# Sorting the second mixture's experts earlier in the program, and one layer 1 output ahead of the weight subtractions

## The chip, the cores and the metric

The kernel runs on one core of one Trainium2 chip. The metric is the device time of one execution in microseconds; the figure for a kernel is the median of several runs. In the profile PE is the matrix engine TensorE (PEld its weight loads), DVE is VectorE, ACT is ScalarE, POOL is GpSimd, and SP issues most of the weight transfers.

## The reference, cut to what matters

An attention without softmax comes first, then two mixtures of eight experts, each of which sends every token to one expert:

```python
kv = np.einsum('bhsd,bhse->bhde', k, v)
out = np.einsum('bhsd,bhde->bhse', q, kv)          # then an RMS norm: x, 2304 tokens of 512
...
xc = x[x @ w_skip > 0]                             # first mixture: the others pass unchanged
e_idx = np.argmax(xc @ w_gate, axis=1)             # gate_w is the softmax at e_idx
for e in range(8):
    h = np.maximum(xc[mask] @ w1[e], 0.0)          # 512 to 1024
    y[mask] = gate_w[mask, None] * (h @ w2[e])     # 1024 to 512
out[do_compute] = xc + y
...
# second mixture: all tokens again, its own gate and weights, a capacity for each expert
h = np.maximum(np.einsum('ecd,edf->ecf', disp, w1), 0.0)
y = np.einsum('ecf,efd->ecd', h, w2)
out[i] = gate_w[i] * y[expert_idx[i], pos[i]]
```

## The kernel before, in words

The rows of all tokens lie in DRAM (`xcat`). A mixture works through eight **slots**; each slot is one expert, the experts sorted by how many tokens they have, and holds up to a fixed number of tokens (`CAP1`, `CAP2`: 384 to 272 in the second mixture). For a slot, POOL gathers the token rows with indirect DMAs of 128 rows (`gather`, L426, index table `gi`), PE transposes them, layer 1 makes `hp` in PSUM, ACT and DVE take it out, layer 2 follows, and POOL scatters the result.

The second mixture multiplies with numbers split in two: ACT casts the high part (`whi` of a weight, `xh` of a row, `hh` of a hidden value), DVE subtracts to get the low part (`wlo` L1159 or L1304, `xl`, `hl` L1330), and PE makes three products (L1310 to L1312). A weight half is 128 x 2048 floats (1,048,576 bytes) in one of six buffers `wraw`; it is cast and subtracted in four pieces of 512 columns.

The expert with most tokens, the **lead**, is known ahead of the others, and its slot 0 runs early, at the end of the first mixture. `l1_early(fc)` makes the eight parts of its layer 1 for the first 256 tokens, and `h_early` takes two parts out at a time. `lead_tokens` makes the index table of its last 128 tokens, `t2_rest` gathers and transposes those, and `l1_rest` makes their layer 1 (L1377) in four pairs of parts. All these `hp` share a pool `p1h` of two PSUM buffers, so the fourth pair of `l1_rest` can start only when the second has been taken out by both ACT (`hh`, L1329) and DVE (`hl`, L1330). Between the early parts stand the last slot's bookkeeping matmuls: `next(todo)` and `run(todo)` step through `add_tokens`, which adds the last tokens to the tables in the PSUM tile `acc` (L1073): A and Bo to the index table `ips2`, U and V to `ups`, which only the overflow path at the end uses.

`sort_experts` then orders the other seven experts, `by_slot` makes their index tables, and `slot_reg` loads the order into the queues. After that `fetch2` may gather the rows of the next slot (three gathers on POOL) and load its four weight halves; for the slot next after the lead these loads stand on POOL's queue behind the gathers, for the others on SP's.

Only PE's order is the order of the code (`manual_schedule`). On DVE, ACT, POOL and SP a scheduler orders the instructions by priority, which follows the code, and by when it thinks them ready; `behind(a, b)` forces `a` after `b`. On the chip each engine then runs its list in that order.

In the first mixture's last slot (j = 7) layer 1 is `l1(j, fp)` for fp 0 to 3. Its outputs for odd fp are taken out by DVE (L711). Right behind the last of them stand `t2_early` (transposes of the lead's first rows, `xl` L1324) and `split2(0, 0)`, the first weight half of the lead, then layer 2, `l2` (L737).

Of the kernel before, what the change touches and what calls it, by code (L numbers as in the profile page):

```python
# [11 lines left out]
ALU = mybir.AluOpType  # L12
# [31 lines left out]
def blocks(n):  # L44
    return [(r, min(128, n - r)) for r in range(0, n, 128)]
# [3 lines left out]
def moe_kernel(ctx: ExitStack, tc: tile.TileContext, qT, kk, vv, aux, w1a, w2a, w1b, w2b, capacity, out):  # L49
    nc = tc.nc  # L50
# [264 lines left out]
    def run(gen):  # L315
        for _ in gen or ():
            pass
# [89 lines left out]
    def slot_reg(order, j, both):  # L407
        eng = [mybir.EngineType.SP] + ([mybir.EngineType.Pool] if both else [])
        return nc.values_load(order[0:1, j:j + 1], engines=eng, min_val=0, max_val=E - 1,
                              skip_runtime_bounds_check_because="the index of an expert")  # L410
# [243 lines left out]
    W, X, XT, HT, YT, GT, EV, YP, LG, YR, XC = {}, {}, {}, {}, {}, {}, {}, {}, {}, {}, {}  # L654
# [28 lines left out]
    def l1(j, fp, c0=0, c1=None, early=False, ffs=(0, 1)):  # L683
        n = CAP1[j]
        c1 = c1 or n
        if fp == 0 and c0 == 0:
            HT[j] = m1.tile([128, 8, 2, n], F32R, name="hT1") if j in SPLIT1 else m1.tile([128, 8, c1], F32, name="hT1")
        if fp == 0 and c0 > 0:
            HT[j] = [m2s.tile([128, 8, c1 - c0], F32R, name=i) for i in ("hh", "hl")]
        if 0 in ffs:  # L690
            YP["hp"] = p1h.tile([128, 2, c1 - c0], F32, name="hp1")
        hp = YP["hp"]
        for ff in ffs:
            fc = fp * 2 + ff
            wv = W[j][fc // 4].rearrange("p (f k m) -> p f k m", f=4, k=4)
            for k in range(4):
                nc.tensor.matmul(hp[:, ff, :], lhsT=wv[:, fc % 4, k, :], rhs=XT[j][:, k, c0:c1], start=(k == 0), stop=(k == 3))  # L697
        if 1 not in ffs:
            return
        if j in SPLIT1:  # L700
            hh, hl = (HT[j][:, 2 * fp:2 * fp + 2, i, :] for i in range(2))
            EV[j] = nc.scalar.activation(out=hh, in_=hp, func=AF.Relu)
            ev = nc.vector.scalar_tensor_tensor(out=hl, in0=hp, scalar=0.0, in1=hh.bitcast(F32), op0=ALU.max, op1=ALU.subtract)
        elif c0 > 0:
            hh, hl = (h[:, 2 * fp:2 * fp + 2, :] for h in HT[j])
            EV[j] = nc.scalar.activation(out=hh, in_=hp, func=AF.Relu)
            EV["rest"] = nc.vector.scalar_tensor_tensor(out=hl, in0=hp, scalar=0.0, in1=hh.bitcast(F32), op0=ALU.max, op1=ALU.subtract)
        elif fp % 2 == 0 or j == 0:
            EV[j] = nc.scalar.activation(out=HT[j][:, 2 * fp:2 * fp + 2, c0:c1], in_=hp, func=AF.Relu)
        else:  # L710
            ev = nc.vector.tensor_scalar(out=HT[j][:, 2 * fp:2 * fp + 2, c0:c1], in0=hp, scalar1=0.0, scalar2=None, op0=ALU.max)  # L711
        if fp == 1 and not early:
            GT[j] = sm.tile([128, NB1], F32, name="g1")
            for bi, (r0, nn) in enumerate(blocks(n)):
                gates(GT[j][:, bi:bi + 1], X[j][bi], nn, D, (None, EV[j]) if j == 0 else (ev, EV[j]))
# [348 lines left out]
    with first_mix:  # L1064
# [86 lines left out]
        def split(raw, after=None, first=None):  # L1151

            hi, lo = pair()
            for c in range(0, 2048, SPLIT):
                cs = slice(c, c + SPLIT)
                ins = nc.scalar.copy(out=hi[:, cs], in_=raw[:, cs])  # L1156
                if first is not None:
                    behind(ins, first)
                ins = nc.vector.tensor_tensor(out=lo[:, cs], in0=raw[:, cs], in1=hi[:, cs].bitcast(F32), op=ALU.subtract)  # L1159
                if after is not None:  # L1160
                    behind(ins, after)
            return hi, lo
# [121 lines left out]
        def split2(j, pc, after=None):  # L1284
            if j in ROWS2 and pc >= 2:
                rows_split(j, pc, after)
            else:
                WS[j, pc] = split(W2[j][pc], after)
# [48 lines left out]
        def l1_early(fc):  # L1337
            xh, xl = XT2[0]
            if fc == 0:
                h_tiles(0)  # L1340
            if fc % 2 == 0:
                YP["h"] = p1h.tile([128, 2, 256], F32, name="hp1")
            hp = YP["h"]
            wv = [w.rearrange("p (f k m) -> p f k m", f=4, k=4) for w in WS[0, fc // 4]]
            for k in range(4):
                mm3(hp[:, fc % 2, :], [w[:, fc % 4, k, :] for w in wv], (xh[:, k, :], xl[:, k, :]), k == 0, k == 3)
            YP["h", fc // 2] = hp

        def h_early(fp):
            ev = h_out(0, YP["h", fp], slice(2 * fp, 2 * fp + 2), slice(0, 256))  # L1350
            if fp == 3:
                GT2[0] = sm.tile([128, NB2], F32, name="g2")
                for bi in range(2):
                    gates(GT2[0][:, bi:bi + 1], X2[0][bi], 128, D + 8, ev)

        def t2_rest():
            n = CAP2[0] - 256
            (x,), _ = load_x(n, r2["gi"], 0, 2)
            X2[0].append(x)
            tp = p1t.tile([128, 4, n], F32, name="tp1")  # L1360
            for dc in range(4):
                nc.tensor.transpose(tp[:, dc, :], x[:n, dc * 128:dc * 128 + 128], ident[:n, :n])
            xB = m2s.tile([128, 4, n], F32, name="xB")
            nc.scalar.copy(out=xB[:, 0:2], in_=tp[:, 0:2])
            nc.vector.tensor_copy(out=xB[:, 2:4], in_=tp[:, 2:4])
            XT2["rest"] = xB

        def l1_rest():
            n = CAP2[0] - 256
            xB = XT2["rest"]  # L1370
            for fp in range(4):
                hp = p1h.tile([128, 2, n], F32, name="hp1")
                for ff in range(2):
                    fc = 2 * fp + ff
                    wv = W2[0][fc // 4].rearrange("p (f k m) -> p f k m", f=4, k=4)
                    for k in range(4):
                        nc.tensor.matmul(hp[:, ff, :], lhsT=wv[:, fc % 4, k, :], rhs=xB[:, k, :], start=(k == 0), stop=(k == 3))  # L1377
                ev = h_out(0, hp, slice(2 * fp, 2 * fp + 2), slice(256, CAP2[0]))
                if fp == 0:
                    gates(GT2[0][:, 2:3], X2[0][2], n, D + 8, ev)  # L1380
# [15 lines left out]
        for j in range(1, E):  # L1396
            l1(j, 0)
            if j == 1:
                rest_turned()
                others_table()  # L1400
                l1(j, 1)
                logits(0)
                back(0, bis=1)
            else:
                logits(j - 1)
                l1(j, 1)
                back(j - 1)
            todo = back_logits(j - 1)
            next(todo)
            l1(j, 2)  # L1410
            if j == 1:
                XC["half"] = EV[j]
            l1(j, 3)
            split1(j, 2)
            split1(j, 3)
            if j + 1 < E:
                t1(j + 1)
            else:
                t2_early()
                split2(0, 0)  # L1420
            l2(j, 0)
            if j < E - 1:
                next(todo)
            l2(j, 1)
            next(todo)
            if j < E - 1:
                run(todo)
            if j == E - 2:
                early([g for i in range(j) for g in SC[i]])
            if j == E - 1:  # L1430
                split2(0, 1)
                split2(0, 2)
            l2(j, 2)
            if j == E - 2:
                add(cnt2, identb, bump)
            l2(j, 3)
            if j + 2 < E:
                fetch1(j + 2)
# [5 lines left out]
        todo = back_logits(E - 1, True)  # L1444
# [4 lines left out]
        l1_early(2)  # L1449
        next(todo)  # L1450
        lead_tokens(r2, ips2, EQ0, slice(2, 3))
        l1_early(3)
        h_early(1)
        l1_early(4)
        run(todo)
        l1_early(5)
        h_early(2)
        l1_early(6)
        t2_rest()
        l1_early(7)  # L1460
        h_early(3)

        ends = rt.tile([128, E], F32, name="ends")
        nc.vector.tensor_copy(out=ends, in_=cnt2)
        key = rt.tile([128, E], F32, name="key_2")
# [2 lines left out]
        sort_experts(r2, key)  # L1468
        by_slot(r2, ips2.rearrange("p e q b -> p e (q b)"), 1, E)
        reg2 = [None] + [slot_reg(r2["order"], j, j == ORDER2[1]) for j in range(1, E)]  # L1470
        l1_rest()
        nc.vector.tensor_tensor(out=OH2, in0=OHk, in1=ups, op=ALU.add)

# [178 lines left out]
```

## Time and profile before

| what | us |
|---|---|
| median of three runs | 482.91 (482.81 to 484.09) |
| the profiled execution | 483.77 |
| its span in the trace | 482.0 |
| PE busy in the span | 464.6 |

The span is what the trace's times count in, from 0; the profiled execution is 1.77 us longer than its span. A row of a timeline gives start, duration, engine, line, operation, out<-in, count, and in brackets how long the engine stood idle ahead of it and what ended that.

### The profile page before, as it was taken

How to read it: one execution, taken by the hardware profiler on the slowest of the kernel's cores; microseconds unless marked ns; L12 is line 12 of the kernel's file. 1: busy time of each engine (PE TensorE's matmuls, PEld its weight loads, DVE VectorE, ACT ScalarE, POOL GpSimd, SP SyncE). 2: the span in 40 equal slices, each digit the busy share in tenths (PEclk: the TensorE clock that was granted, in tenths of full speed). 3: DMA queues.
4: the chain of work that ended last, by engine and by line, in shares of the span. 5: the costliest groups of instructions: out<-in, count | busy, mean ns of one | idle time of the engine just before them, and what ended most of it. 6: DMA issues, size and time to landing. Idle time of an engine off the chain costs nothing.

```text
span 482.0 us, 10172 instructions
## 1 busy us (share of the span) xinstructions
PE 464.6 (96%) x3797; PEld 440.3 (91%) x3797; DVE 304.3 (63%) x964; ACT 206.9 (43%) x514; POOL 143.5 (30%) x177
## 2 busy tenths in 40 slices
PE   7999987999999999999999999999999999999995
PEld 3888987899999999999888999999999999999985
DVE  2367778986776755439683764756657566776611
ACT  1574663455344231126232553554544544555400
POOL 5585955011302123111261410501506033030201
PEclk9999999999999999999999999999999999999999
DMA  8998958989776965565149965554656566310101
GB/s 280 410 407 299 355 214 275 371 306 312 291 258 211 326 185 195 179 253 205 45 134 420 345 242 175 200 184 154 225 175 196 186 239 209 103 38 0 38 22 41
DMA packets 21386, 104.88 MB, mean 218 GB/s; under 512 B 3323, under 2 KB 3451, under 8 KB 12626
## 3 DMA queue, kind: packets, MB, share of 16 engines
q1 hardware_dynamic: 14032, 76.70, 44.9%
q0 software_dynamic: 7152, 27.40, 16.6%
q8 instruction: 31, 0.51, 0.4%
q14 instruction: 25, 0.20, 0.1%
q10 hardware_dynamic: 146, 0.07, 0.1%
HBM read 92.15 MB, written 12.76 MB: 218 GB/s over the span
## 4 chain that ended last, share of the span: by engine, by line
PE 73%; DVE 6%; DMA 3%; issue 1%; ACT 0%; POOL 0%; POOLq 0%; SPq 0%; ACTq 0%
PE hp L697 12%; PE yp L1310 8%; PE yp L1312 8%; PE yp L1311 8%; PE yp L727 6%; PE hp L1310 6%; PE hp L1311 6%; PE hp L1312 6%; PE yp L728 2%; PE yp L737 2%; PE yt L1545 2%; PE tp L1501 2%; DVE wlo L1159 2%; DMA wraw<-in_w1b 1%; PE tp L677 1%; DMA rows<-xcat,gi 1%
## 5 line engine op out<-in xcount | busy, mean ns | idle before, releaser
L1156 ACT CAST whi<-wraw 128x512 fp32r<-128x512 f32 x152 | 86.0, 619 | 77.8 <-PE yp L1311 30.1
L1159 DVE TENSOR_TENSOR wlo<-wraw,whi 128x512 fp32r<-128x512 f32 x152 | 97.3, 685 | 28.7 <-ACT whi L1156 27.6
L426 POOL DMA_INDIRECT rows<-xcat,gi x40 | 42.2, 1056 | 148.6 <-ACT ex L435 86.1
L1310 PE MATMUL hp<-xh,whi 128*128 128x256 f32 (+7 forms) x256 | 78.8, 308 | 0.3 <-DVE hl L1330 0.3
L1312 PE MATMUL hp<-xh,wlo 128*128 128x256 f32 (+7 forms) x256 | 76.7, 299 | 0.0
L1311 PE MATMUL hp<-xl,whi 128*128 128x256 f32 (+7 forms) x256 | 76.6, 299 | 0.0
L697 PE MATMUL hp<-xT,wraw 128*128 128x148 f32 (+8 forms) x544 | 73.5, 291 | 1.5 <-ACT base L1139 1.5
L697 PEld LDWEIGHTS hp<-xT,wraw 128*128 128x128 f32 x544 | 69.8, 190 | 3.2 <-ACT base L1139 1.6
L1535 POOL DMA_INDIRECT out<-ot,toki x24 | 34.7, 1446 | 84.6 <-DVE su L439 39.5
L1310 PE MATMUL yp<-hh,whi 128*128 128x320 f32 (+5 forms) x192 | 58.8, 306 | 0.0
L1312 PE MATMUL yp<-hh,wlo 128*128 128x320 f32 (+5 forms) x192 | 57.3, 298 | 0.0
L1311 PE MATMUL yp<-hl,whi 128*128 128x320 f32 (+5 forms) x192 | 57.3, 298 | 0.0
L1310 PEld LDWEIGHTS hp<-xh,whi 128*128 128x128 f32 x256 | 48.2, 188 | 0.9 <-DVE hl L1330 0.8
L1311 PEld LDWEIGHTS hp<-xl,whi 128*128 128x128 f32 x256 | 48.3, 189 | 0.0
L1312 PEld LDWEIGHTS hp<-xh,wlo 128*128 128x128 f32 x256 | 48.3, 189 | 0.0
L727 PE MATMUL yp<-hT,whi 128*128 128x352 f32 (+4 forms) x160 | 43.1, 350 | 0.0
L1217 POOL DMA_INDIRECT xcat<-rows,toki x16 | 16.3, 1020 | 84.5 <-DVE mxt L382 82.1
L1329 ACT ACTIVATE hh<-hp 128x320 fp32r<-128x320 f32 (+8 forms) x64 | 27.1, 428 | 32.7 <-PE hp L1312 25.1
L1330 DVE SCALAR_TENSOR_TENSOR hl<-hp,hh 128x320 fp32r<-128x320 f32 (+8 forms) x64 | 30.1, 477 | 13.8 <-ACT hh L1329 12.5
L728 PE MATMUL yp<-hT,wlo 128*128 128x176 f32 (+4 forms) x160 | 37.7, 236 | 0.0
L1311 PEld LDWEIGHTS yp<-hl,whi 128*128 128x128 f32 x192 | 36.2, 188 | 0.0
L1310 PEld LDWEIGHTS yp<-hh,whi 128*128 128x128 f32 x192 | 36.1, 188 | 0.0
(308 smaller groups left out, 856.0 us busy)
## 6 DMA issues: line engine op xcount, KB each, us to landing
wraw<-in_w2a SPq DMA_DIRECT2D x14, 1024.0 KB
wraw<-in_w1b SPq DMA_DIRECT2D x14, 1024.0 KB
wraw<-in_w2b SPq DMA_DIRECT2D x14, 1024.0 KB
wraw<-in_w1a SPq DMA_DIRECT2D x13, 1024.0 KB
xcat<-xa SPq DMA_DIRECT2D x18, 264.0 KB
q<-in_q SPq DMA_DIRECT2D x4, 1152.0 KB
wraw<-in_k SPq DMA_DIRECT2D x8, 512.0 KB
wraw<-in_v SPq DMA_DIRECT2D x8, 512.0 KB
```

The lines of the kernel that those rows point to most:

```text
L426: return nc.gpsimd.indirect_dma_start(out=rows[:n], out_offset=None, in_=xcat[0:source], in_offset=bass.IndirectOffsetOnAxis(ap=gi[:n], ax ...
L697: nc.tensor.matmul(hp[:, ff, :], lhsT=wv[:, fc % 4, k, :], rhs=XT[j][:, k, c0:c1], start=(k == 0), stop=(k == 3))
L727: nc.tensor.matmul(yp, lhsT=wh[:, fc, :], rhs=HT[j][:, fc], start=(fc == 0), stop=False, skip_group_check=True)
L728: nc.tensor.matmul(yp[:, 0, :], lhsT=wl[:, fc, :], rhs=HT[j][:, fc, 0, :], start=False, stop=(fc == 7), skip_group_check=True)
L1156: ins = nc.scalar.copy(out=hi[:, cs], in_=raw[:, cs])
L1159: ins = nc.vector.tensor_tensor(out=lo[:, cs], in0=raw[:, cs], in1=hi[:, cs].bitcast(F32), op=ALU.subtract)
L1310: nc.tensor.matmul(ps, lhsT=wh, rhs=xh, start=first, stop=False)
L1311: nc.tensor.matmul(ps, lhsT=wh, rhs=xl, start=False, stop=False)
L1312: nc.tensor.matmul(ps, lhsT=wl, rhs=xh, start=False, stop=last)
L1329: ea = nc.scalar.activation(out=hh[:, fs, cs], in_=hp, func=AF.Relu)
L1330: ev = nc.vector.scalar_tensor_tensor(out=hl[:, fs, cs], in0=hp, scalar=0.0, in1=hh[:, fs, cs].bitcast(F32), op0=ALU.max, op1=ALU.subtract)
L1535: st = nc.gpsimd.indirect_dma_start(out=out, out_offset=bass.IndirectOffsetOnAxis(ap=r2["toki"][:nn, j, bi:bi + 1], axis=0), in_=ot[:nn], ...
```

## The change

Two edits. `sort_experts`, `by_slot` and the register loads move ahead of the lead's parts 3 to 7 and the gather of its last tokens, right behind `lead_tokens`; the U and V additions (`run(todo)`) go behind part 5. And the last odd output of layer 1 of the last slot (`EV["odd"]`) is handed to `split2(0, 0)`, so that the subtractions of that weight half come behind it on DVE.

```diff
@@ l1 @@
-            ev = nc.vector.tensor_scalar(out=HT[j][...], in0=hp, scalar1=0.0, scalar2=None, op0=ALU.max)
+            ev = EV["odd"] = nc.vector.tensor_scalar(out=HT[j][...], in0=hp, scalar1=0.0, scalar2=None, op0=ALU.max)
...
                 t2_early()
-                split2(0, 0)
+                split2(0, 0, EV["odd"])
...
         lead_tokens(r2, ips2, EQ0, slice(2, 3))
-        l1_early(3)
-        h_early(1)
-        l1_early(4)
-        run(todo)
-        l1_early(5)
-        h_early(2)
-        l1_early(6)
-        t2_rest()
-        l1_early(7)
-        h_early(3)
-
         ends = rt.tile([128, E], F32, name="ends")
...
         reg2 = [None] + [slot_reg(r2["order"], j, j == ORDER2[1]) for j in range(1, E)]
+        l1_early(3)
+        h_early(1)
+        l1_early(4)
+        l1_early(5)
+        run(todo)
+        h_early(2)
+        l1_early(6)
+        t2_rest()
+        l1_early(7)
+        h_early(3)
+
         l1_rest()
```

**On DVE, around the last odd output (L711 of hp_3468).** Here `xl` is the low part of the lead's rows, `wlo` of its weights, A, Bo and V are the tables of the slot before.

```order
+L1116 TENSOR_TENSOR V<-hv,o_1_1243 128x144
 L711 TENSOR_SCALAR hT_3375<-hp_3468 128x272
-L387 TENSOR_SCALAR o_1_1243<-sct,m2t,valid_1612 128x8
+L1159 TENSOR_TENSOR wlo<-wraw,whi 128x512 x2
 L1324 TENSOR_TENSOR xl<-tp_3480,xh 128x512
 L1324 TENSOR_TENSOR xl<-tp_3487,xh 128x512
```

The five L1159 that stood ahead of this L711 in the order (two of them even ahead of the first odd output) are now behind it, two at once and the rest behind `xl`. From there to the copy L741 that layer 2 needs, the list before reads

```order
L1109 TENSOR_TENSOR Bo<-o_1_1243,tab_207 128x16 x2
L1116 TENSOR_TENSOR V<-hv,o_1_1243 128x144 x2
L1159 TENSOR_TENSOR wlo<-wraw,whi 128x512 x3
L1101 TENSOR_TENSOR rk_3529<-lg,base 128x16
L1304 TENSOR_TENSOR wlo<-wraw,whi 128x4x128
L1102 TENSOR_TENSOR rk_3529<-rk_3529,o_1_1243 128x16
L1304 TENSOR_TENSOR wlo<-wraw,whi 128x4x128
L1104 TENSOR_REDUCE rk<-rk_3529 128x2
L1108 TENSOR_SCALAR A_3534<-row_99,rk 128x384 x2
L741 COPY yT_3504<-yp_3565 128x272
```

and now

```order
L1159 TENSOR_TENSOR wlo<-wraw,whi 128x512 x4
L1101 TENSOR_TENSOR rk_3529<-lg,base 128x16
L1159 TENSOR_TENSOR wlo<-wraw,whi 128x512
L1102 TENSOR_TENSOR rk_3529<-rk_3529,o_1_1243 128x16
L1159 TENSOR_TENSOR wlo<-wraw,whi 128x512
L1104 TENSOR_REDUCE rk<-rk_3529 128x2
L1304 TENSOR_TENSOR wlo<-wraw,whi 128x4x128
L1108 TENSOR_SCALAR A_3534<-row_99,rk 128x384 x2
L1304 TENSOR_TENSOR wlo<-wraw,whi 128x4x128
L741 COPY yT_3504<-yp_3565 128x272
```

Between `xl` and A there stand seven weight subtractions instead of five, and an eighth between A and the copy L741.

**On DVE, the sort.** Right behind the token tables of the lead the list is now as follows; before, the take-out `hl<-hp_3693` stood ahead of `ends`, `hl<-hp_3732` and L1472 inside the chain.

```order
L358 TENSOR_SCALAR toki_1237<-tok_1236 128x1
L341 TENSOR_TENSOR G_3723<-key_3720 128x64
L346 TENSOR_REDUCE slot_3725<-G_3723 128x8
L348 TENSOR_TENSOR EQ_3727<-rowf,slot_3725 128x64
L330 TENSOR_TENSOR oe_3729<-EQ_3727,rowf 1x64
L366 TENSOR_TENSOR T_2_1_3735<-acc,EQ_3727 128x336
L332 TENSOR_REDUCE of_3731<-oe_3729 1x8
L370 TENSOR_REDUCE tab_1235<-T_2_1_3735 128x42
L334 CAST order_3733<-of_3731 1x8
L1330 SCALAR_TENSOR_TENSOR hl<-hp_3693,hh 128x2x256
L356 SCALAR_TENSOR_TENSOR tok_1236<-tab_1235 128x21
L357 TENSOR_SCALAR gi_1238<-tok_1236 128x21
```

The three short operations on `ends` and `key` ahead of G now alternate with the lead's token operations.

**On ACT, in the stretch of `l1_rest`.** hp_3860, hp_3878, hp_3889 and hp_3900 are its four pairs; the casts L1156 are those of the first weight half of the next slot, which POOL loads.

```order
 L1329 ACTIVATE hh<-hp_3860 128x2x128
 L435 ACTIVATE ex,su<-rows,nx 128x8
+L1156 CAST whi<-wraw 128x512
 L1329 ACTIVATE hh<-hp_3878 128x2x128
+L1156 CAST whi<-wraw 128x512 x3
 L1329 ACTIVATE hh<-hp_3889 128x2x128
-L1156 CAST whi<-wraw 128x512 x2
 L1329 ACTIVATE hh<-hp_3900 128x2x128
 L1502 CAST xh<-tp_3987 128x320
-L1156 CAST whi<-wraw 128x512 x2
```

The casts stood behind the third take-out; now one stands ahead of the second take-out and three ahead of the third. DVE's list follows: one `wlo` L1159 ahead of `hl<-hp_3878`.

## Rows read from the trace of the kernel before

**Rows 1.** The page, part 1: busy time, share of the span, instructions.

```profile
PE 464.6 (96%) x3797; PEld 440.3 (91%) x3797; DVE 304.3 (63%) x964; ACT 206.9 (43%) x514; POOL 143.5 (30%) x177
```

**Rows 2.** PE's waits from 253 us to the end: total us, times, longest.

```profile
PE tp L1501 <- DMA rows<-xcat,gi: 1.2, 1, 1.2
PE hp L1310 <- DVE hl L1330: 0.3, 1, 0.3
```

**Rows 3.** Windows: length, busy us by engine, PE clock, DMA share, GB/s.

```profile
249.00:250.00 1.00, 1.00 (x10) 0.83 (x9) 0.86 (x6) 0.43 (x2) 1.00 (x3) 1.00 0.91 177
256.00:257.00 1.00, 1.00 (x6) 0.82 (x5) 0.16 (x1) 0.81 (x2) 0.00 (x0) 1.00 1.04 434
...
280.00:300.00 20.00, 20.00 (x142) 19.97 (x141) 10.60 (x20) 8.57 (x20) 0.00 (x0) 1.00 0.54 184
```

**Rows 4.** The chain that ended last, its one step on a DMA here.

```profile
247.25 6.04 DMA rows<-xcat,gi
```

**Rows 5.** Timeline of PE, layer 2 of the last slot.

```profile
220.61 1.55 PE L737 MATMUL yp<-hT,wraw 128*128 128x136 f32 x12
222.84 2.58 PE L737 MATMUL yp<-hT,wraw 128*128 128x136 f32 x20 [0.67 <-DVE hT L711]
...
229.99 0.44 PE L1177 MATMUL lg<-yT,wg2w 128*32 128x136 f32 x8
```

**Rows 6.** Timeline of DVE in that stretch.

```profile
222.37 0.42 DVE L711 TENSOR_SCALAR hT<-hp 128x272 f32<-128x272 f32 x1
...
224.10 0.24 DVE L1109 TENSOR_TENSOR Bo<-o,tab 128x16 bf16<-128x16 bf16 x2
...
224.71 1.88 DVE L1159 TENSOR_TENSOR wlo<-wraw,whi 128x512 fp32r<-128x512 f32 x3
...
228.07 0.75 DVE L1108 TENSOR_SCALAR A<-row,rk 128x384 bf16<-128x384 f32 x2
229.38 0.44 DVE L741 COPY yT<-yp 128x272 f32<-128x272 f32 x1 [0.56 <-PE yp L737]
```

**Rows 7.** Timeline of ACT: first weight half and rows of the lead.

```profile
215.43 2.18 ACT L1156 CAST whi<-wraw 128x512 fp32r<-128x512 f32 x4 [2.05 <-DMA wraw<-in_w1b]
...
222.18 1.07 ACT L1323 CAST xh<-tp 128x512 fp32r<-128x512 f32 x2
```

**Rows 8.** Timeline of DVE: token tables of the lead, then the sort.

```profile
236.54 0.17 DVE L639 TENSOR_TENSOR lt<-acc,lead_2l 128x16 f32<-128x16 f32 x1 [0.33 <-PE acc L1073]
...
239.75 0.16 DVE L1464 COPY ends<-acc 128x8 f32<-128x8 f32 x1
...
243.56 0.18 DVE L357 TENSOR_SCALAR gi<-tok 128x21 int32<-128x21 f32 x1
```

**Rows 9.** Timeline of POOL: the next slot's first gather and first weight loads.

```profile
244.61 1.04 POOL L426 DMA_INDIRECT rows<-xcat,gi  x1 [5.38 <-PE hp L1312]
...
248.25 1.18 POOL L414 DMA_DIRECT2D wraw<-in_w1b  x2
```

**Rows 10.** Timeline of PE, `l1_rest` and what follows it.

```profile
244.24 7.70 PE L1377 MATMUL hp<-xB,wraw 128*128 128x128 f32 x64
251.78 0.38 PE L1501 MATMUL tp<-ident,rows 128*128 128x128 f32 x2
253.33 0.33 PE L1501 MATMUL tp<-ident,rows 128*128 128x128 f32 x1 [1.18 <-DMA rows<-xcat,gi]
253.42 0.48 PE L1310 MATMUL yp<-whi,hh 128*128 128x512 f32 x1
```

**Rows 11.** Timeline of ACT: the next slot's first casts.

```profile
256.19 1.15 ACT L1156 CAST whi<-wraw 128x512 fp32r<-128x512 f32 x2 [5.86 <-DMA wraw<-in_w1b]
```

**Rows 12.** Timeline of DVE behind those casts.

```profile
256.84 1.29 DVE L1159 TENSOR_TENSOR wlo<-wraw,whi 128x512 fp32r<-128x512 f32 x2 [5.37 <-ACT whi L1156]
258.06 0.42 DVE L1330 SCALAR_TENSOR_TENSOR hl<-hp,hh 128x256 fp32r<-128x256 f32 x1
```

**Rows 13.** Timeline of SP: loads of the lead's first weight halves.

```profile
208.93 2.24 SPq L414 DMA_DIRECT2D wraw<-in_w1b  x2
```

More of the change, by code (lines that the diff above doesn't have):

```diff
@@ L710, in l1 @@
         else:
-            ev = nc.vector.tensor_scalar(out=HT[j][:, 2 * fp:2 * fp + 2, c0:c1], in0=hp, scalar1=0.0, scalar2=None, op0=ALU.max)
+            ev = EV["odd"] = nc.vector.tensor_scalar(out=HT[j][:, 2 * fp:2 * fp + 2, c0:c1], in0=hp, scalar1=0.0, scalar2=None, op0=ALU.max)
         if fp == 1 and not early:
```

## The prediction

> **What bounds the kernel now.** The page's busy times come first: PE is busy for 464.6 of 482.0 us [rows 1], and what it lacks is to be looked for wait by wait. From 253 us to the end PE's waits list 0.3 us and one wait of 1.2 us [rows 2], and a window of 20 us there is filled by PE to 20.00 [rows 3]: whatever PE loses or gains before 253 us reaches the end of the kernel one for one, as nothing behind it can take it back. The chain that ended last leaves PE here for one step, 6.04 us in the DMA of a gather issued at 247.25 [rows 4]. PE's timeline shows the same place: its last transpose of the next slot's rows stands until 253.33 for the rows [rows 10]. A second wait lies earlier: layer 2 of the last slot stands 0.67 us for the odd output L711 [rows 5]. The two edits meet these two waits. So I look at what else is moved with them, and where on DVE and ACT it comes to stand.
>
> The sum counts in the times of the profiled execution, whose span is 482.0 and whose time is 483.77, 1.77 more. That is 0.86 above the median of 482.91; I add the difference that comes out to the median.
>
> **The odd output.** L711 ends at 222.37 + 0.42 = 222.79 [rows 6], and PE had nothing left to multiply from 220.61 + 1.55 = 222.16 [rows 5]. With the three L1159 between 217 and 222 us gone from its front and the four short table operations in their place, L711 comes about 1.2 us earlier and the 0.67 us are saved. But the subtractions aren't gone. The `xl` pair can't start earlier than before, since ACT casts `xh` only from 222.18 to 223.25 [rows 7], so DVE goes on behind it at 224.10 as before [rows 6]. Then there stood, up to A, the four short operations (224.10 to 224.71) and five subtractions; now there stand seven. Three L1159 take 1.88 together, overlapping a little, 0.60 each at their pace; A moves back by 2 x 0.60 - 0.61 = 0.6 us to about 228.65, and the copy L741, behind the eighth subtraction, to 228.65 + 0.7 + 0.60 = 229.95 where it began at 229.38. The logits (L1177, at 229.99) need that copy, so they come 0.4 to 0.6 us later though layer 2 came earlier; a little of that was slack. I take **+0.4 us** for this edit. Its bounds are -0.67 (the wait goes and DVE keeps up) and +0.7 (each subtraction at the full 0.63).
>
> **The sort.** Before, `ends` began at 239.75 and the index table `gi` was done at 243.56 + 0.18 = 243.74 [rows 8], 3.99 us with one `hl` and L1472 (about 0.2) inside. Now it starts in the gaps of the token operations that begin at 236.54, at about 236.6; the `hl` is still inside and L1472 not. So `gi` is done near 236.6 + 3.8 = 240.4, 3.3 us earlier. POOL starts its gather 0.87 us after `gi` (243.74 to 244.61) and the weights 3.64 after that, at 248.25 [rows 9]. Moved by 3.3 us that is a first gather at 241.3 and the first weight half issued at 244.9. The third gather then starts at 247.25 - 3.3 = 243.95; even with its 6.04 us the rows land at 250.0, before the transposes that want them at 251.78 [rows 10]. The wait is gone: the three transposes take about 0.29, layer 2 would start at 252.07, and it started at 253.42, so **-1.35 us**. The U and V additions only change places on PE, for nothing.
>
> **What comes in its place.** The scheduler has put the next slot's first cast ahead of the take-out of `l1_rest`'s second pair on ACT, and the matching `wlo` ahead of its `hl` on DVE. Before, these casts started at 256.19, and 5.86 us of waiting for the weights stood ahead of them [rows 11]; two take-outs of `l1_rest` had already gone by. Now that wait stands in front of the second take-out. The fourth pair of `l1_rest` needs the PSUM buffer of the second. Its 64 matmuls begin at 244.24 and what follows at 251.78, 0.118 us each [rows 10]; the fourth pair starts with the 49th, at 249.9. It can now start only when the weight half has landed, has been cast in one piece, subtracted in one piece, and `hl` is out: 256.19 to 256.84 for the cast, 0.61 for the `wlo` (1.22 for two until the next starts) and 0.42 for `hl` [rows 11, 12], 1.7 us in all.
>
> So how long is it from issue to cast? The trace has the same kind of half twice: issued at 208.93 on SP, cast at 215.43 as soon as it came [rows 7, 13], 6.5 us; issued at 248.25 on POOL, cast at 256.19 [rows 9, 11], 7.9 us, the latter beside a load of SP's. In the change the load follows three gathers as before and SP's next load isn't yet free to start, as its buffer is read by `l1_rest`; I take 7.0. Then the cast is at 244.9 + 7.0 = 251.9, the fourth pair at 253.6, and PE has stood 253.6 - 249.9 = **+3.7 us**. With 6.5 it is 3.2, with 7.9 it is 4.6. From below there is only what the bytes allow: 1.05 MB at the best rate of a window, 434 GB/s [rows 3], are 2.4 us, and then no stall is left.
>
> Here the Trainium skill speaks for less. "DMA: Bandwidth & Descriptors", section on the anatomy of a DMA on the SWDGE (gpsimd) path, gives 2.0 us plus the bytes over 436 GB/s for one DMA, as an estimate 4.4 us for this half; by that the stall would be 1.1 us and the kernel would come out at 483.0. The two loads of this trace, 6.5 and 7.9 us, don't agree with it, and the sum goes by them.
>
> Behind the stall, ACT does the other casts and take-outs in at most 3 us, while PE has 1.9 us of the fourth pair and the transposes; the next slot's later weights come later by the same few us and find a PE that waits for nothing there [rows 2], so I charge nothing more.
>
> **The sum**: +0.4 - 1.35 + 3.7 = +2.75 us, 482.91 + 2.75 = 485.7 us.
>
> **The rivals.**
> 1. *The weights land sooner, and the new wait only pays back the old* (same). The point is a landing that costs the stall about 1 us: cast by 249.2, 4.3 us after the issue, gives 250.9 - 249.9 = 1.0 and a sum of 0.4 - 1.35 + 1.0 = +0.05, 483.0. For it: nothing of SP's shares the DMA engines then. Against it: in the window right behind the issue they were 91% busy at only 177 GB/s [rows 3], with the gathers still ahead of the weights. Any landing of 3.3 to 5.7 us stays within 0.3%. The 4.4 us worked out from the Trainium skill's page above lie here.
> 2. *The new wait doesn't form* (not slower): the half lands within 3.3 us of its issue, by 248.2, and ACT has passed its cast before PE wants the buffer. Then 0.4 - 1.35 = -0.95 is left, 482.0, which can't be told from no change; only if DVE keeps up as in rival 3 does it become faster, -2.0 and 480.9. For it speaks only the 2.4 us of the bytes; against it both loads.
> 3. *DVE keeps up at the odd output*: -0.67 in place of +0.4. With the new wait that gives 482.91 - 0.67 - 1.35 + 3.7 = 484.6, still slower.
> 4. *The half lands late*, 8.5 us after its issue, because SP's load comes in between: a stall of 5.2, +4.25 and 487.2.
>
> **How the numbers follow.** About 0.3%, 1.45 us, is what a measurement of this kernel can tell from no change. Forecast with rivals 3 and 4 (a landing of more than 5.75 us): 0.81. Rival 1: 0.13. Rival 2: 0.06, half of it with rival 3's gain and so faster. That is 0.81 slower, 0.16 within and 0.03 faster. The range reaches from a landing of 5.4 us (stall 2.1, +1.15, 484.1) to one of 8.3 (stall 5.0, +4.05, 487.0).
>
> **What would show it.** In the changed profile: PE's wait at L737 for L711 gone and A or L741 waited for instead; the first gather of the next slot near 241.7 and its weights issued near 245.3 (both with the 0.4); no wait of PE for the rows at L1501; and a wait of some 3.7 us at L1377, put down to DVE's `hl` or, behind that, to ACT's cast that waited for `in_w1b`. If ACT's cast starts by 249 us, the step on the landing is wrong and the kernel is no slower; if L1177 isn't later than 229.99, the step on the subtractions is.

## The result: 1.2% slower, and the clock fell behind the new wait

| | before | after |
|---|---|---|
| median of the runs, us | 482.86 (482.08 to 484.09, 4 runs) | 488.60 (487.09 to 490.10, 4 runs) |
| ratio, 95% interval | | 1.0116 (1.0074 to 1.0158) |
| the profiled execution, us | 483.77 | 490.10 |
| its span | 482.0 | 488.3 |
| first matmul of `l1_early` to first of the next slot's layer 2, us | 231.06 to 253.42, 22.36 | 231.38 to 259.37, 27.99 |

The direction was right and the size too small: 485.7 was predicted, 487.0 was the range's end. The last line of the table is the measure of the stretch that the change moves; behind it before needs 482.0 - 253.42 = 228.6 us and after 488.3 - 259.37 = 228.9, so all but 0.3 of the 6.3 us of span are lost ahead of 259.37.

PE's longest waits of after, by what ended them, with total, times and longest:

```profile
PE hp L1377 <- DVE hl L1330: 5.1, 1, 5.1
PE acc L835 <- DMA wraw<-in_v: 3.0, 2, 2.3
PE tp L677 <- DMA rows<-xcat,gi: 1.6, 1, 1.6
```

The waits for L711 and for the rows at L1501 [rows 2, 5] are gone, and one of 5.1 us is new; the other two stand ahead of 80 us, in code that isn't changed. PE's timeline shows the new one ahead of the fourth pair of `l1_rest`:

```profile
244.64 5.54 PE L1377 MATMUL hp<-xB,wraw 128*128 128x128 f32 x48
255.30 3.78 PE L1377 MATMUL hp<-xB,wraw 128*128 128x128 f32 x16 [5.12 <-DVE hl L1330]
258.87 0.85 PE L1501 MATMUL tp<-ident,rows 128*128 128x128 f32 x3
259.37 0.78 PE L1310 MATMUL yp<-whi,hh 128*128 128x512 f32 x1
260.55 0.39 PE L1310 MATMUL yp<-whi,hh 128*128 128x512 f32 x1
```

ACT and POOL, in their timelines, tell what it waits for. ACT takes out the first pair, then stands with the cast of the next slot's weights ahead of it; POOL had issued them behind three gathers:

```profile
246.98 0.36 ACT L1329 ACTIVATE hh<-hp 128x256 fp32r<-128x256 f32 x1
...
253.56 0.62 ACT L1156 CAST whi<-wraw 128x512 fp32r<-128x512 f32 x1 [5.18 <-DMA wraw<-in_w1b]
254.09 0.38 ACT L1329 ACTIVATE hh<-hp 128x256 fp32r<-128x256 f32 x1
```

```profile
241.73 1.30 POOL L426 DMA_INDIRECT rows<-xcat,gi  x1 [2.10 <-PE acc L1073]
...
245.95 1.20 POOL L414 DMA_DIRECT2D wraw<-in_w1b  x2
```

So the chain is weights issued at 245.95, landed and cast at 253.56, `hl` out, fourth pair at 255.30: the predicted one, at its end 1.3 us later than the 253.6 + 0.4 of the prediction. What wasn't predicted stands in the same rows. Sixteen matmuls took 3.78 us where a quarter of the 64 of before took 1.9 [rows 10]. The windows (length, busy us of PE, its weight loads, DVE, ACT and POOL, granted PE clock, DMA share, GB/s) say why:

```profile
250.00:253.00 3.00, 0.18 (x2) 0.00 (x0) 0.00 (x0) 0.00 (x0) 1.89 (x2) 1.00 0.97 404
253.00:254.00 1.00, 0.00 (x0) 0.00 (x0) 0.00 (x0) 0.43 (x1) 0.00 (x0) 0.70 1.01 426
254.00:260.00 6.00, 4.70 (x21) 4.61 (x22) 3.58 (x7) 2.86 (x8) 0.00 (x0) 0.50 1.01 426
260.00:261.00 1.00, 1.00 (x5) 0.83 (x4) 0.49 (x1) 0.24 (x1) 0.00 (x0) 0.89 0.96 406
```

While PE stood idle its clock was granted at 0.50, the lower of its two levels (1.2 of 2.4 GHz), and it stayed there beyond 260 us: 0.89 in the last window is 0.22 us at 0.50 and the rest at 1.00, so PE's first 4.9 us of work, 255.30 to 260.22, ran at the lower level. In before the windows read are at 1.00 [rows 3].

### The profile page after: what moved, and what is told of

Same layout as the page of the kernel before. It is cut to its first block, busy times and chain, and to the rows that moved or that the text cites. A ratio compares the mean times of both kernels' runs of the same rounds, so it can differ in the third digit from the quotient of the medians.

```text
span 488.3 us, 10174 instructions
## 1 busy us (share of the span) xinstructions
PE 465.9 (95%) x3797; PEld 442.4 (91%) x3797; DVE 304.4 (62%) x964; ACT 207.0 (42%) x514; POOL 141.2 (29%) x177
## 4 chain that ended last, share of the span: by engine, by line
PE 75%; DVE 5%; DMA 2%; issue 1%; POOLq 0%; POOL 0%; ACT 0%; DVEq 0%; ACTq 0%
PE hp L697 13%; PE yp L1310 8%; PE yp L1311 8%; PE yp L1312 8%; PE yp L727 6%; PE hp L1310 6%; PE hp L1312 6%; PE hp L1311 6%; PE yp L737 3%; PE yp L728 2%; PE tp L1501 2%; PE yt L1545 2%; DMA wraw<-in_w1b 2%; PE tp L1190 1%; PE tp L677 1%; PE yp L1234 1%
## 5 line engine op out<-in xcount | busy, mean ns | idle before, releaser
L1156 ACT CAST whi<-wraw 128x512 fp32r<-128x512 f32 x152 | 86.0, 619 | 72.8 <-PE yp L1311 30.1
L1159 DVE TENSOR_TENSOR wlo<-wraw,whi 128x512 fp32r<-128x512 f32 x152 | 97.2, 685 | 22.4 <-ACT whi L1156 21.3
L1310 PE MATMUL hp<-xh,whi 128*128 128x256 f32 (+7 forms) x256 | 78.8, 308 | 0.3 <-DVE hl L1330 0.2
L697 PE MATMUL hp<-xT,wraw 128*128 128x148 f32 (+8 forms) x544 | 73.8, 291 | 0.9 <-DVE U L1118 0.4
L697 PEld LDWEIGHTS hp<-xT,wraw 128*128 128x128 f32 x544 | 69.9, 190 | 2.8 <-issue 2.1
L1535 POOL DMA_INDIRECT out<-ot,toki x24 | 32.3, 1344 | 93.2 <-DVE ot L1565 43.1
L1310 PE MATMUL yp<-hh,whi 128*128 128x320 f32 (+5 forms) x192 | 58.8, 306 | 0.0
L1310 PEld LDWEIGHTS hp<-xh,whi 128*128 128x128 f32 x256 | 48.2, 188 | 0.9 <-DVE hl L1330 0.8
L1310 PEld LDWEIGHTS yp<-hh,whi 128*128 128x128 f32 x192 | 36.1, 188 | 0.0
```

Source lines behind the costliest of these rows:

```text
L1310: nc.tensor.matmul(ps, lhsT=wh, rhs=xh, start=first, stop=False)
L1535: st = nc.gpsimd.indirect_dma_start(out=out, out_offset=bass.IndirectOffsetOnAxis(ap=r2["toki"][:nn, j, bi:bi + 1], axis=0), in_=ot[:nn], ...
```

## The experiments

Each was compared with the kernel before on its own chip. "Stretch" is the last line of the table above, in each run's own profiled execution; it leaves out what other parts of the kernel do to an execution. The ratio with its interval is worked out from all the single executions; it need not be the quotient of the two medians. A median stands for several executions and a stretch for one of them: e9's profiled execution took 485.32 us, the shortest of its four, and the other three took 487.0 to 487.9.

| kernel | stretch, us | PE's wait ahead of the fourth pair | its 16 matmuls, us | median, us | before there | ratio, interval |
|---|---|---|---|---|---|---|
| before | 22.36 | none | 1.9 | 482.86 | | |
| after | 27.99 | 5.12 | 3.78 | 488.60 | 482.86 | 1.0116 (1.0074 to 1.0158) |
| e1 sort alone | 28.08 | 5.31 | 3.78 | 489.47 | 482.72 | 1.0112 (1.0051 to 1.0172) |
| e2 odd output alone | 21.29 | none | 1.9 | 483.27 | 482.72 | 0.9994 (0.9958 to 1.0030) |
| e3 casts back | 20.67 | none | 1.9 | 482.65 | 482.72 | 0.9988 (0.9957 to 1.0020) |
| e3 again | 20.58 | none | 1.9 | 481.04 | 482.13 | 0.9969 (0.9937 to 1.0001) |
| e5 sort, casts back | 20.66 | none | 1.9 | 481.10 | 482.13 | 0.9975 (0.9945 to 1.0004) |
| e4 22 added matmuls | 25.42 | filled | 1.95 | 486.53 | 482.72 | 1.0072 (1.0041 to 1.0102) |
| e7 the same again | 25.43 | filled | 1.95 | 486.12 | 482.13 | 1.0076 (1.0039 to 1.0112) |
| e8 11 added | 27.34 | 2.49 | 3.63 | 487.98 | 481.96 | 1.0125 (1.0081 to 1.0169) |
| e9 5 added | 24.66 | 2.74 | 2.05 | 487.11 | 481.96 | 1.0112 (1.0092 to 1.0131) |
| e6 weights on SP | 23.53 | none | 1.9 | 485.47 | 482.13 | 1.0058 (1.0025 to 1.0092) |

(1.9 stands where the 64 matmuls ran without a break.)

**The two edits apart.** e1 is after without the odd output's edit, e2 is before with that edit alone.

```diff
-            ev = EV["odd"] = nc.vector.tensor_scalar(out=HT[j][...], in0=hp, ..., op0=ALU.max)
+            ev = nc.vector.tensor_scalar(out=HT[j][...], in0=hp, ..., op0=ALU.max)
...
-                split2(0, 0, EV["odd"])
+                split2(0, 0)
```

> The changed kernel with only the moved sort and tables; the odd output of the last slot stands where it stood before the change. Theory (the stall ahead of the fourth pair of the last slot's layer 1, which waits for the cast of the second mixture's weights, and the clock that falls after it, make the whole loss): stall of 4.5 to 5.5 us ahead of the 16 matmuls of L1377, granted clock near 0.5 behind it, time about 488, at most 0.4 below the changed kernel. Rival (the output moved ahead of the subtractions makes the loss): no stall, about 482 to 483.

> The kernel before with only the last slot's odd output moved ahead of the subtractions. Theory (VectorE falls two subtractions behind, TensorE's wait moves from hT to A): +0.3 to +0.4, about 483.2, within 0.3% of before. Rival (VectorE keeps up and the 0.67 us wait is saved): 482.2. Second rival (this edit makes the loss): 486 or more.

e1 has the whole loss, the wait and the low clock; e2 has none of it. The loss is the moved sort's. e2 has no wait for rows at L1501 either, though its sort stands where it stood: its third gather was issued at 250.62 and PE's transposes ran through at 255.07. So the wait of 1.18 us [rows 10] that the change was to save belongs to some executions of the old order.

**The order on ACT.** e3 is after, with the next slot's first casts and subtractions held behind the last take-out of `l1_rest`; the sort, the gathers and the loads stay early. The first added line stands in `l1_rest`, behind each take-out.

```diff
+                EV["rest out"] = ev
...
-                        split2(nxt[0], i - 1)
+                        split2(nxt[0], i - 1, *(() if p else EV["rest out"]))
```

> The changed kernel, with the first casts and subtractions of the second mixture's weights held behind the last take-out of the last slot's layer 1 on ScalarE and VectorE, so that no take-out waits for a weight transfer. Theory (the order on ScalarE makes the stall, and the stall makes the clock fall): no wait ahead of the fourth pair, granted clock 1.00 from 250 to 262, the gathers' wait still gone: 482.9 + 0.4 - 1.35 = 482, faster than both kernels by a little. Rival (the gathers and the weights that now run earlier take DMA bandwidth, or the clock falls for another reason): stays at 486 or more.

The wait is gone, with the gathers and the loads as early as in after: in both the first gather begins 10.3 us behind the first matmul of `l1_early` and the first weights are issued 14.6 us behind it. PE's timeline of e3, with its matmuls and rows unbroken (its L1502 is L1501 of after):

```profile
246.10 7.33 PE L1377 MATMUL hp<-xB,wraw 128*128 128x128 f32 x64
253.27 0.49 PE L1502 MATMUL tp<-ident,rows 128*128 128x128 f32 x3
253.52 0.48 PE L1310 MATMUL yp<-whi,hh 128*128 128x512 f32 x1
```

and ACT's, where the cast follows the four take-outs and waits 0.56 us, which costs PE nothing (it is busy for 3.00 of the 3.00 us from 253 to 256):

```profile
253.47 0.38 ACT L1329 ACTIVATE hh<-hp 128x256 fp32r<-128x256 f32 x1 [1.41 <-PE hp L1377]
254.41 0.62 ACT L1156 CAST whi<-wraw 128x512 fp32r<-128x512 f32 x1 [0.56 <-DMA wraw<-in_w1b]
```

The stretch falls from 27.99 to 20.67, the time by 6 us. So the order on ACT makes the stall, and its rival (early gathers and weights cost bandwidth) falls, as they are as early here. That the total only equals before's is settled by the next runs.

> The same kernel as the run that held the casts back, again, with more rounds. Theory: 20.7 us from the first matmul of l1_early to the first of layer 2 (22.4 before), so 0.7 to 1.7 us faster than the kernel before between executions that are alike up to 220 us; the wait of TensorE near 78 us, in code that no edit touches, makes some executions 2 to 3 us longer. Rival (the gain of the gathers is noise): ratio at 1.000 or above.

> The moved sort with the first casts of the second mixture's weights held behind the last take-out, as in the run that held them back, but with the last slot's odd output where it stood before the change. Theory (the odd output is worth nothing or costs up to 0.4, the sort alone brings the gain): no wait ahead of the fourth pair, 20.7 us or a little less from the first matmul of l1_early to the first of layer 2, median 481.5 to 482.6. Rival (the odd output carries the gain): like the kernel before, 22.4 us there and 482.8.

e5 is e3 without the odd output's edit, e3 again the same kernel as e3. Both came out about 1.1 us under the before of their chip, with intervals that just reach no change; the stretch is 1.7 us shorter than the profiled one of before, 0.7 shorter than e2's, which had no wait for rows (its 64 matmuls and the three transposes took 7.62 and 0.81 us, 7.34 and 0.49 in e3 again). These are the best versions found. The window of 256 to 262 us in e3 again shows PE full and its clock granted in full:

```profile
256.00:262.00 6.00, 6.00 (x31) 5.02 (x30) 1.64 (x3) 0.75 (x2) 1.03 (x1) 1.00 1.02 430
```

**The clock.** e4 is after with matmuls on zeros between the third and the fourth pair, which write a PSUM buffer that nobody reads; the wait stays and PE works through it. It adds work and leaves out none; e8 has 11 of them and e9 has 5.

```diff
+                if fp == 3:
+                    warm(p1y.tile([128, 512], F32, name="yp1"), 22)
                 hp = p1h.tile([128, 2, n], F32, name="hp1")
```

> The changed kernel with 22 added matmuls of 512 columns on zeros, whose output nobody reads, on TensorE between the third and the fourth pair of the last slot's layer 1, where it stands idle. Theory (TensorE's idle time makes its clock fall, and the fall costs about 2.3 us): the fourth pair still starts near 255.3, with granted clock 1.00, its 16 matmuls take about 1.9 us instead of 3.8, and the time falls by about 2.3 us. Rival (what stands behind the stall is slow for another reason, such as the operands): no change, or slower by the added matmuls.

The stretch is 2.57 us shorter than in after. Of these, 2.04 are the clock's: from the fourth pair to layer 2 PE takes 255.94 - 253.91 = 2.03 us, where after takes 259.37 - 255.30 = 4.07. The first three matmuls of layer 2 take 0.76 instead of 1.18, so in all the clock costs 2.46 us. The other 0.53 of the stretch come from a shorter wait: the half was cast 6.8 us after its issue here, 7.6 in after. The ratios agree, 1.0072 and 1.0076 (e4, e7) against 1.0116 and 1.0112 (after, e1), some 2 us of 483, but their intervals overlap, so it is the profiles that show the price. PE's timeline of e4 and one of its windows:

```profile
249.16 4.91 PE L112 MATMUL yp<-zb 128*128 128x512 bf16 x22
253.91 1.95 PE L1379 MATMUL hp<-xB,wraw 128*128 128x128 f32 x16
```

```profile
254.00:260.00 6.00, 6.00 (x38) 5.31 (x37) 2.58 (x6) 1.40 (x4) 0.00 (x0) 1.00 1.02 426
```

e7 was meant to carry 11 of these matmuls and carried 22, so it is e4 once more, and gave the same; its expectation is that of e8, which does carry 11.

> The changed kernel with 11 added matmuls on zeros in place of 22 between the third and the fourth pair, so that half of TensorE's idle time is filled and about 2.7 us stay idle. Theory (the length of the idle time decides whether the clock falls, and when): granted clock between that of the changed kernel (0.50 behind the stall) and 1.00, time between 486.5 and 488.6. Rival (any idle time of over a microsecond or two makes it fall as far): fourth pair still at 3.8 us, time 488.6.

> The changed kernel with 11 added matmuls of 512 columns on zeros between the third and the fourth pair (half of those of the run with 22), so that about 2.5 of the 5.1 us stay idle. Theory (how long TensorE stands idle decides whether, and when, the clock falls): granted clock in 250 to 262 between the 0.72 of the changed kernel and 1.00, the fourth pair's 16 matmuls between 3.8 and 1.95 us, time between 486.1 and 488.6. Rival (work on TensorE before the idle time does not matter, it falls as far as without): 3.8 us, 488.6.

> The changed kernel with 5 added matmuls on zeros at the same place, so that about 3.9 of the 5.1 us stay idle. Theory: the clock falls, later than in the changed kernel if at all later: fourth pair 3 to 3.8 us, time 487.5 to 488.6. Rival (a few matmuls are enough to keep it): fourth pair 1.95 us, 486.1.

e8 by itself agrees with the theory, and e9 turns it round: PE was idle 2.49 us in e8 and its clock fell; it was idle 2.74 us in e9, with fewer matmuls ahead of that, and it didn't. PE's timelines of e8 and, below it, of e9:

```profile
254.29 3.63 PE L1379 MATMUL hp<-xB,wraw 128*128 128x128 f32 x16 [2.49 <-DVE hl L1330]
```

```profile
253.21 2.05 PE L1379 MATMUL hp<-xB,wraw 128*128 128x128 f32 x16 [2.74 <-DVE hl L1330]
```

Two more profiles, of the same programs as after and e8, show that at this length it isn't the program that decides:

> The changed kernel once more, for its profile alone. Theory (with a wait of 5 us the clock falls each time): wait of 4.5 to 5.5 us ahead of the fourth pair, granted clock 0.50 behind it, the fourth pair's 16 matmuls 3.8 us. Rival (whether it falls changes from execution to execution, as the mean clocks of 0.990 and 0.996 of its executions suggest): the same wait, clock 1.00, 2.0 us, a time near 487.

> The kernel with 11 added matmuls once more, for its profile alone. Theory (a wait of 2.5 us makes the clock fall in some executions and not in others): either the clock stays at 1.00 here and the fourth pair takes 2.0 us, or it falls again. Rival (the 11 matmuls ahead decide, and 5 would not make it fall): it falls again at the same place, 3.6 us.

After again waited 4.93 us and had its clock at 0.50 behind it (3.78 us for the 16 matmuls, stretch 27.81); e8 again waited 2.69 us and kept it. The same window in e8 and, below it, in e8 again:

```profile
254.00:258.00 4.00, 3.71 (x18) 3.71 (x19) 2.37 (x5) 1.33 (x4) 0.00 (x0) 0.57 1.01 426
```

```profile
254.00:258.00 4.00, 4.00 (x28) 3.65 (x28) 2.77 (x6) 1.58 (x4) 0.00 (x0) 1.00 1.01 428
```

One program with nearly the same idle time paid once and not the other time. In the three profiles with waits of about 5 us (after, after again, e1) it paid each time; what decides in between stays open. Nor is it shown that every execution of after paid as much: the mean clocks of its four are 0.990 and 0.991 at 490.10 and 489.49 us, but 0.996 at 487.71 and 487.09, and no profile shows the last two.

**When the weights land.** e6 issues the next slot's weights on SP as soon as the order is known, instead of on POOL behind the gathers (POOL's load of that register goes with them); ACT's order is left as in after.

```diff
-        W2[j] = [load_w(w, hf, reg2[j], *((nc.gpsimd, G[-1]) if j == ORDER2[1] else (nc.sync,))) for ...]
+        W2[j] = [load_w(w, hf, reg2[j], nc.sync) for ...]
```

> The changed kernel with the weights of the second mixture's next slot issued on SyncE's queue as soon as the slot's index is known, not on GpSimd's behind the gathers; the cast still stands ahead of the second pair's take-out. Theory (the stall is as long as the issue and the landing of these weights leave it): issued 4 to 5 us earlier, landing 6.5 to 8 us later, the cast at 248 to 250, stall 0 to 1.5 us, granted clock 1.00, time 482 to 484. Rival (the weights and the gathers share the bandwidth, so that the half lands at the same time): cast near 253.5, stall near 5 us, time 488.

The wait ahead of the fourth pair is gone, as the cast came at 247.39, 6.7 us after the issue. But another took its place. SP's and POOL's timelines, a step of the chain that ended last, and PE's:

```profile
240.67 0.91 SPq L414 DMA_DIRECT2D wraw<-in_w1b  x2
```

```profile
244.88 1.23 POOL L426 DMA_INDIRECT rows<-xcat,gi  x1 [0.31 <-issue]
```

```profile
244.88 10.06 DMA rows<-xcat,gi
```

```profile
254.98 0.33 PE L1501 MATMUL tp<-ident,rows 128*128 128x128 f32 x1 [2.60 <-DMA rows<-xcat,gi]
```

The third gather took 10.06 us instead of 6.04 [rows 4] beside the weight halves on SP; the three gathers landed 8.1 to 10.1 us after their issue here and 3.7 to 5.4 in e5. PE stood 2.6 us for it, and its clock was at 0.50 from 257 to 259 us. The time of 485.5 is 1.5 above what was expected at most. The theory holds for the wait that it was about and missed the gathers. The Trainium skill ("DMA: Bandwidth & Descriptors", section on SWDGE, HWDGE and iDMA) says that the two kinds of DMA, POOL's and SP's here, feed different queues inside each DMA engine, which serves them in turn. The trace agrees as far as it goes: SP's weights and POOL's gather were under way together, and the gather took 4 us longer. That the taking of turns is what held it up isn't shown.

## Where the prediction was right, and the step that failed

**The odd output, +0.4.** Right in mechanism; the size varies. In after L711 begins 1.3 us earlier than before (1.2 predicted), A starts at 228.58, L741 at 229.84 (229.95 predicted), and `l1_early` 0.32 us later than before. DVE's timeline of after and, below it, the `xl` of before:

```profile
221.04 0.43 DVE L711 TENSOR_SCALAR hT<-hp 128x272 f32<-128x272 f32 x1
...
222.92 1.29 DVE L1324 TENSOR_TENSOR xl<-tp,xh 128x512 fp32r<-128x512 f32 x2 [0.25 <-ACT xh L1323]
...
228.58 0.75 DVE L1108 TENSOR_SCALAR A<-row,rk 128x384 bf16<-128x384 f32 x2
...
229.84 0.44 DVE L741 COPY yT<-yp 128x272 f32<-128x272 f32 x1
```

```profile
222.91 1.27 DVE L1324 TENSOR_TENSOR xl<-tp,xh 128x512 fp32r<-128x512 f32 x2
```

`xl` waits for ACT's `xh`, as argued, and starts no earlier than before. In all eleven profiles with the edit L741 starts 6.9 us behind `xl`, in the three without it (before, e1, e5) 6.4 to 6.5: the added subtractions cost DVE 0.4 to 0.55 us, as argued. How much of that PE feels changes. After can't tell it by itself: PE had come 1 us later into this stretch than before, behind a longer wait for `in_v` among others (3.0 us in all, 1.9 before), so that its 0.32 meets the predicted 0.4 partly by chance. In e5 and e3 again layer 2 begins at 220.69 and 220.62 and `l1_early` at 230.21 and 230.65: 0.5 us for the edit. In e2, which has it too, `l1_early` begins 9.51 us behind layer 2, as in e5 (9.52): nothing. The gain has no fixed size either: in e5 the wait for L711 wasn't there at all, since its weights were cast from 214.32 and not from 215.43 [rows 7], nor was it in e1, so the 0.67 us of [rows 5] belong to one of the three profiles of the old order. At the end of the kernel the edit can't be seen (481.04 and 481.10).

**The sort, -1.35.** Right in its times: `gi` was done at 240.86 (240.4 predicted, 240.8 with the 0.4), the first gather began at 241.73 (241.7), and the wait at L1501 is gone. With the new wait taken away (e3, e5) the stretch shrinks by 1.7 us; but e2 shows that 1.1 of that can be had by chance.

**What comes in its place, +3.7.** Right in mechanism, undersized by 1.4: the issue came 0.65 us later than predicted and the landing took 0.6 longer. The three gathers took POOL from 241.73 to 245.95, 4.2 us where 3.6 were carried over from before, and the half was cast 7.6 us after its issue (7.0 taken, 7.9 the upper end). From cast to fourth pair it took 1.74 us (1.7). In the ten profiles of the moved sort in which this cast waited for this load it came 6.3 to 7.8 us after the issue (e9, e5), so the wait's size changes from execution to execution by itself, and 7.0 lies about in the middle.

**Behind the stall, "I charge nothing more".** This is the step that failed. From the fourth pair to layer 2 PE took 259.37 - 255.30 = 4.07 us; at the full clock 16 x 0.118 + 0.29 = 2.18 were to be had, and the first three matmuls of layer 2 lost another 0.4 (1.18 us until L1310 comes again, where it was 254.20 - 253.42 = 0.78 in before [rows 10]): 2.3 us. That it is the clock e4 shows: the same work takes 2.46 us less there. By "TensorE: Matmul & The Clock Gate" of the Trainium skill (section on how the oscillation bites in real kernels) half of the time worked at the lower clock is lost; as an estimate that is half of 4.9, 2.45 us, and the trace agrees. The 4.9 are read from after's profile and weren't known beforehand; but the sum put this term at nothing after looking only at ACT, at the transposes and at the later weights, and not at the clock.

**The sum.** 0.32 - 1.35 + 5.12 + 1.9 = 5.99 us up to layer 2, against 259.37 - 253.42 = 5.95. Without the clock's 1.9 it is +4.1 and 487.0, the end of the range; without the 1.4 of the stall as well, +2.7, the number predicted. Rivals 1 and 2 (the half lands soon enough) are out: none of those ten profiles had it in under 6.3 us, and the 4.4 us that the prediction gave as an estimate lie below them all. Rival 3 is out in after, where DVE didn't keep up; only in e2 did PE lose nothing. Rival 4 had the size of the wait, 5.2 us, partly by luck: the half took 7.6 us and not 8.5, but was issued later. Half of its reason was there: SP's next load was issued at 248.54, 5 us before the cast, where the prediction took 7.0 because that load wasn't yet free to start. How much it delayed the half wasn't tried.

## What to carry to other kernels

When an early load lets a scheduler place its first consumer, look where that consumer stands in its engine's queue: a cast that waits for a transfer holds up every take-out behind it, and it can be tied behind the last of them for nothing. Price a new stall of PE with its clock as well: here 5 us of waiting cost over 2 us more. And before a wait of a microsecond is charged as a gain, see in a second execution whether it is always there.

## What was not expected of the hardware

The clock fell behind idle times of PE of 1.90, 2.49, 2.56 and 2.60 us (e3, e8, e2, e6) and not behind 1.46, 2.1, 2.46, 2.50, 2.69 and 2.74 us (before, e9, e1, e6, e8 again, e9): from 1.9 to 2.7 us the length of a wait doesn't tell.

Five of these, 1.90 in e3, 2.56 in e2, 2.46 in e1, 2.1 in e9 and before's 1.46, are one wait ahead of L697 near 78 us, in code that no edit touches. It differs from execution to execution and goes with the spread of the times: of e3 again's 12 executions, the nine with a mean clock of 0.996 or more took 480.2 to 481.6 us, the three at 0.993 and 0.994 took 483.4 to 484.0. The window of 80 to 85 us in e3's profile, and below it in e3 again's, where that wait was 0.45 us:

```profile
80.00:85.00 5.00, 5.00 (x35) 5.00 (x35) 4.09 (x16) 1.00 (x5) 0.38 (x1) 0.72 0.92 380
```

```profile
80.00:85.00 5.00, 4.58 (x42) 4.41 (x41) 5.00 (x21) 1.56 (x7) 1.12 (x2) 1.00 1.02 404
```

e3's profiled execution took 483.9 us and e3 again's 480.77, with stretches of 20.67 and 20.58 us later on. For a change worth one microsecond here, the stretch measured in the profile says more than the median.
